# First batch's phi, keys and values as six tokens on each of 96 partitions, queries as pairs, one order on two engines; W1's means taken off by products

## The chip, the core and the metric

The kernel runs on one core of a Trainium2 chip. A core has TensorE (PE, matrix products into PSUM), VectorE (DVE), ScalarE (ACT), GpSimd (POOL) and SyncE (SP), whose queue here issues every load and store; 16 DMA engines carry them out. The metric is the device time of one execution in microseconds, the median of several runs.

## The reference

Three layers in a row, for 8 batches of 576 tokens. Attention over 32 memory slots a head, a layer norm with a two-layer network added to it, and a gated layer that mixes tokens:

```
a = softmax over the 576 tokens of phi          # 8 x 8 heads x 576 x 32
k_m, v_m = a^T k, a^T v                         # 32 x 64 a head
x = softmax(q k_m^T / 8) v_m                    # heads side by side: 576 x 512
xn = (x - mean(x)) / sqrt(var(x) + 1e-6) * g_ln
x = x + relu(xn @ w_ch1) @ w_ch2                # 512 -> 2048 -> 512
h = gelu(x @ w_in); u, v = halves of h          # 512 -> 1024
x + (u * (w_sg @ (layernorm(v) * g) + b_sg)) @ w_out
```

The weight matrices reach the chip as 64-bit floating-point numbers; q, k, v and phi are 32-bit.

## The kernel before

**Phase 1** takes the batches one behind the other; the second layer follows in phase 2, which the change does not touch. Since x is attention weights times v_m, the product of x with W1 is taken as attention weights times VW, where VW = v_m times W1. For that W1 is scaled by g_ln and its column means are taken off (`center_w1`: TensorE makes the means with a constant column, L505, DVE subtracts them in two instructions of 1024 elements a partition, L507). W1 has four quarters of 512 columns (`fb` 0 to 3), and the hidden layer runs quarter by quarter: six products make `ph` (L593, `m1`), ACT takes relu (`hh`, L579), DVE the rounding rest (`hl`, L580, and `cr` for the odd 64 tokens), and three steps later `m2` multiplies with W2 (L623 to L625).

**Weights** arrive as 64-bit words (`raw`, 128 x 512, runs of 4 KB). A tile is turned into 32-bit numbers by ACT on the upper words (L114) and DVE with a shift (L115) and a shift-or (L116). W1's are then scaled by ACT into `wc` (L499), W2's are split by ACT and GpSimd into a high and a low half (L128, L129). The centred W1 is stored to `w_d` by `store_w1` and read back by later batches (`load_wc`).

**The first batch** has nothing to stand beside. Phi, keys and values are loaded with 4 tokens a partition (512 of 576 tokens on 128 partitions, runs of 512 B) and a remainder of 64 tokens (`prz`, `kvr`). `prep_max` and `prep_exp` (L252 to L278) take the maximum over tokens with transposes on TensorE and the exponential; `prep_sum` adds four tokens and the remainder on GpSimd (L283 to L288) and `turn_sum` transposes the sums; `prep_kv` makes k_m and v_m (L315), `prep_norm` divides by the sums (L335), `prep_T` transposes them (L352). Queries are loaded token by token (runs of 256 B), transposed by TensorE (`t_q`, L376) and copied by ACT (L377). `t_scores` makes scores (L401), DVE transposes them (L410) and takes maxima and differences (L413, L414), ACT the exponential (L415); `t_norm` sums and divides (L421 to L424), `t_attn` transposes again (L429) and writes `aTh` and `aTl` (L440, L441). Tokens come in three groups: two of 256 and one of 64. `make_vw` multiplies v_m with W1 (L545), `evict_vw` splits the result (L551 on ACT, L552 on DVE).

**Order.** Each step is an event `at_time(time, function)` in units of an eighteenth of a batch; events with smaller times are issued earlier, those before -0.4 ahead of the first `ph`. A scheduler then sets each engine's order from the issue order and its own estimate; `tc.issue_after(x)` keeps an instruction behind x. All loads go by `load` (L87) on the SP queue in the issue order: an entry that waits for its buffer holds the ones behind it. From the second batch on, queries are laid out anew in DRAM (`q_d`, three buffers) and transposed by DVE (L379).

## Time and profile before

| | us |
|---|---|
| median of 3 runs | 1204.23 (1202.42 to 1206.30) |
| the profiled execution | 1205.68 |
| its span | 1203.50 |
| TensorE busy in the span | 1170.44 |
| DVE, ACT, GpSimd busy | 688.04, 467.69, 401.85 |

The profiled execution is one run, 1.45 us above the median; 2.18 us of it lie outside the span. All times in rows count from the span's start. Engine columns of a windows row are busy time with the number of instructions in brackets; a number in square brackets at a timeline row is the engine's idle time before it, with what ended it.

### The profile page before, as it was taken

To read this page: it belongs to the slowest core of one execution; us is meant where nothing else is said; L and a number is where in the kernel's file an instruction comes from. 1 tells how busy PE (TensorE), PEld (TensorE's weight loads), DVE (VectorE), ACT (ScalarE), POOL (GpSimd) and SP (SyncE) were. 2 spreads that over 40 slices of the span, in tenths; PEclk is the share of its full clock that TensorE was granted. 3 is DMA by queue.
4 is the path that set the end of the run, shared out by engine and by line. 5 is a ranking of instruction groups with operands and counts; after the bars stand their busy time and mean duration, and the time that the engine had idled before them with its cause. 6 is when DMAs were issued, how large, how long until landed. Compare 5 with 4: busy or idle time off the path is not lost.

```text
span 1203.5 us, 20688 instructions
## 1 busy us (share of the span) xinstructions
PE 1170.4 (97%) x7711; PEld 993.1 (83%) x7711; DVE 688.0 (57%) x1669; ACT 467.7 (39%) x1071; POOL 401.8 (33%) x622
## 2 busy tenths in 40 slices
PE   4899899999999999999999999999999999999998
PEld 3486678788788888788888888889989988998997
DVE  4886665755644645644546445567476377447532
ACT  3665332323332322422333445445444354344430
POOL 2234112311201211201211112456666475566641
PEclk9799899999999999999999999999999999999999
DMA  8984834463341543231410343032240052022201
GB/s 248 354 242 120 236 80 126 93 194 76 97 117 31 146 124 67 92 108 25 126 35 27 108 125 116 27 82 88 82 139 18 19 150 69 2 84 84 79 19 71
DMA packets 198900, 124.14 MB, mean 103 GB/s; under 512 B 93072, under 2 KB 174096, under 8 KB 198800
## 3 DMA queue, kind: packets, MB, share of 16 engines
q1 hardware_dynamic: 198800, 122.82, 35.4%
q8 instruction: 61, 1.00, 0.3%
q14 instruction: 39, 0.32, 0.1%
HBM read 99.72 MB, written 31.33 MB: 109 GB/s over the span
## 4 chain that ended last, share of the span: by engine, by line
PE 88%; DVE 6%; DMA 2%; SPq 1%; ACT 1%; issue 1%; POOL 1%; POOLq 0%; ACTq 0%; DVEq 0%
PE ph L593 16%; PE py L623 10%; PE py L625 10%; PE py L624 10%; PE pvs L1029 9%; PE po L1052 8%; PE pv L920 8%; PE pu L1004 7%; PE pvw L545 3%; DMA q<-q_d 1%; PE kvp L315 1%; SPq L87 1%; PE cm L505 1%; PE px L460 1%; DVE qT L379 1%; PE px L459 1%
## 5 line engine op out<-in xcount | busy, mean ns | idle before, releaser
L593 PE MATMUL ph<-aTh,vw 128*128 128x320 f32 (+1 forms) x1024 | 248.4, 301 | 1.4 <-ACT vw L551 1.4
L623 PE MATMUL py<-whl,hh 128*128 128x512 f32 x512 | 202.3, 397 | 6.7 <-ACT hh L579 6.5
L624 PE MATMUL py<-whl,hh 128*128 128x512 f32 x512 | 201.2, 393 | 0.0
L593 PEld LDWEIGHTS ph<-aTh,vw 128*128 128x128 f32 x1024 | 179.5, 191 | 26.0 <-issue 8.8
L625 PE MATMUL py<-whl,hl 128*128 128x512 f32 x512 | 182.7, 397 | 0.0
L579 ACT ACTIVATE hh<-ph 128x256 fp32r<-128x256 f32 x256 | 96.5, 386 | 168.5 <-PE ph L593 111.0
L580 DVE SCALAR_TENSOR_TENSOR hl<-ph,hh 128x256 fp32r<-128x256 f32 x256 | 106.4, 421 | 91.1 <-ACT hh L579 90.6
L593 PE MATMUL ph<-aTl,vw 128*128 128x256 f32 (+1 forms) x512 | 152.7, 299 | 0.0
L623 PEld LDWEIGHTS py<-whl,hh 128*128 128x128 f32 x512 | 96.5, 189 | 30.1 <-ACT hh L579 8.6
L1029 PE MATMUL pvs<-wsh,vhl 128*128 128x288 f32 x576 | 121.1, 295 | 0.0
L624 PEld LDWEIGHTS py<-whl,hh 128*128 128x128 f32 x512 | 96.7, 189 | 19.0 <-issue 0.5
L1004 PE MATMUL pu<-yTh,whl 128*128 128x288 f32 x512 | 111.0, 296 | 0.2 <-DVE ug L909 0.2
L593 PEld LDWEIGHTS ph<-aTl,vw 128*128 128x128 f32 x512 | 97.7, 191 | 11.2 <-issue 3.6
L625 PEld LDWEIGHTS py<-whl,hl 128*128 128x128 f32 x512 | 90.3, 190 | 11.9 <-issue 2.3
L1029 PEld LDWEIGHTS pvs<-wsh,vhl 128*128 128x128 f32 x576 | 94.4, 189 | 0.7
L920 PE MATMUL pv<-whl,yTh 128*128 128x512 f32 x288 | 91.0, 396 | 0.0
L1052 PE MATMUL po<-whl,gh 128*128 128x512 f32 x288 | 90.1, 391 | 0.0
L1004 PEld LDWEIGHTS pu<-yTh,whl 128*128 128x128 f32 x512 | 85.4, 189 | 1.9 <-DVE ug L909 0.9
L579 ACT ACTIVATE cr<-ph 128x64 fp32r<-128x64 f32 x128 | 28.7, 226 | 126.3 <-PE ph L593 125.7
L1032 POOL TENSOR_TENSOR gt<-gt,ug 128x288 f32<-128x288 f32 x64 | 52.9, 827 | 68.3 <-DVE gt L1031 61.8
L1029 PE MATMUL pvs<-wsl,vhl 128*128 128x288 f32 x256 | 75.6, 295 | 0.0
L1004 PE MATMUL pu<-yTl,whl 128*128 128x288 f32 x256 | 75.5, 295 | 0.0
(154 smaller groups left out, 2164.5 us busy)
## 6 DMA issues: line engine op xcount, KB each, us to landing
raw<-in_moe_w_ch_dram SPq DMA_DIRECT2D x32, 512.0 KB, 7.8
wc<-w_d SPq DMA_DIRECT2D x28, 512.0 KB, 5.7
y_d<-x SPq DMA_DIRECT2D x36, 256.0 KB, 2.2
yt<-y_d SPq DMA_DIRECT2D x36, 256.0 KB, 2.7
yr<-y_d SPq DMA_DIRECT2D x36, 256.0 KB, 2.8
kv<-in_k_dram SPq DMA_DIRECT2D x32, 256.0 KB, 3.9
kv<-in_v_dram SPq DMA_DIRECT2D x32, 256.0 KB, 4.0
out_dram<-yr SPq DMA_DIRECT2D x32, 256.0 KB, 2.0
```

Of the source, the lines that this page charges most:

```text
L545: mm = PE.matmul(ps[g][ms, :], vT[rs_, ms], ws[j // 2][rs_, j % 2, :], start=True, stop=True, skip_group_check=True)
L579: high = A.activation(out_h, src, AF.Relu)
L580: return high, V.scalar_tensor_tensor(out=out_l, in0=src, scalar=0.0, in1=out_h.bitcast(F32), op0=ALU.max, op1=ALU.subtract)
L593: R["ph"] = PE.matmul(ph, w_[:, ks], x[:, g, 0:w], start=(n == 0), stop=(n == 3 * HK - 1))
L623: PE.matmul(py, hh, wh, start=start, stop=False)
L624: PE.matmul(py, hh, wl, start=False, stop=False)
L625: PE.matmul(py, hl, wh, start=False, stop=stop)
L920: PE.matmul(pv, y[:, kc, cs], w, start=(n == 0), stop=(n == 3 * KC - 1))
L1004: PE.matmul(pu, w[:, ds_], y[:, kc, cs], start=(n == 0), stop=(n == 3 * KC - 1))
L1029: PE.matmul(pvs, v_, w_, start=(n == 0), stop=(n == len(ops) - 1))
L1032: G.tensor_tensor(out=gt, in0=gt, in1=ug, op=ALU.mult)
L1052: PE.matmul(po, gg[:, dc, cs], w, start=(n == 0), stop=(n == 3 * KC - 1))
```

## The change

Line numbers of the changed program differ. What it does:

- **Loads.** Batch 0's phi, keys and values come as 6 consecutive tokens on each of 96 partitions, with no remainder: phi in runs of 768 B, keys and values of 1536 B. Queries come as pairs of tokens (runs of 512 B), 256 tokens a load. The tiles lie in a pool of their own (`start`) that `open_tail` closes.
- **Sums.** TensorE adds the exponentials with the constant column (`kv_first`); GpSimd's sums and the transposes are gone.
- **Queries.** They are transposed by products with the identity that write 64 rows each; a strided copy puts the pairs in order.
- **One order.** `behind(gate)` chains the start's work on ACT (`st["act"]`) and DVE (`st["v"]`); the maximum and difference of the scores (`t_soft`) are a step of their own. The second group's query products wait for the first group's scores, the means for the second group's. Second and third group are divided by their sums behind the first VW.
- **Means.** For the first two quarters of W1, ACT writes the negated means (`ncm`) and TensorE adds v_m times `ncm` into the same sums as VW. DVE adds `ncm` to W1 later (`center_late`), ahead of the store. The last two quarters are centred as before, later in the order.
- **Weights.** The first four tiles of W2 are loaded ahead of W1's second quarter; the loads of the fourth quarter, the stores and the centring move to later times.

```diff
+    def behind(gate):
+        es = ExitStack()
+        for ins in gate or ():
+            es.enter_context(tc.issue_after(ins.ins))
+        return es
...
+        def load_kv0(g, n):
+            t = start.tile([P, 2, 2, C0, D], F32, name=f"kv0{g}{n}")
+            for i, src in enumerate((k, v)):
+                load(t[:P0, i], src[0, g, 2 * n:2 * n + 2].rearrange("h (p c) d -> p h c d", c=C0))
...
+        def kv_first(g):
...
+            for c in range(C0):
+                w = ex[:, c].rearrange("p h m -> p (h m)")
+                PE.matmul(st["sums"][:, g:g + 1], w, mcol[:P0], start=(c == 0), stop=(c == C0 - 1), skip_group_check=True)
...
+                elif i % 2 == 0:
+                    t = start.tile([P, H, 2, D], F32, name=f"q0{i}")
+                    load(t, q[b, :, i * P:i * P + 2 * P, :].rearrange("h (p r) d -> p h r d", r=2))
...
+                with behind([first_grs[n_ - 1]["sc"][0]] if n_ else None):
+                    for c in range(4):
+                        if n == P:
+                            for o in range(2):
+                                PE.matmul(pt[64 * o:64 * o + 64, c, :], t[:, 2 * c + o], ident, start=True, stop=True, skip_group_check=True)
...
         def center_w1(fb):
             ws = WC[fb]
             cm = ps_of(fb, [P, DM], "cm")
             for j in range(KC):
-                PE.matmul(cm, mean, ws[j // 2][:, j % 2, :], start=(j == 0), stop=(j == KC - 1))
-            for n in range(2):
-                V.tensor_tensor(out=ws[n], in0=ws[n], in1=cm.unsqueeze(1).to_broadcast([P, 2, DM]), op=ALU.subtract)
+                with behind([first_grs[1]["sc"][0]] if fb == 0 else None):
+                    PE.matmul(cm, mean, ws[j // 2][:, j % 2, :], start=(j == 0), stop=(j == KC - 1))
+            if fb < 2:
+                st["cm", fb] = at.tile([P, DM], F32, tag="at32" if fb else "z", name="ncm")
+                with behind([st["act"]] if fb == 0 else None):
+                    ins = A.mul(st["cm", fb], cm, -1.0)
+                if fb == 0:
+                    st["act"] = ins
+            else:
+                for n in range(2):
+                    V.tensor_tensor(out=ws[n], in0=ws[n], in1=cm.unsqueeze(1).to_broadcast([P, 2, DM]), op=ALU.subtract)
+
+        def center_late(fb):
+            with behind([st["hl"]]):
+                for ws in WC[fb]:
+                    V.tensor_tensor(out=ws, in0=ws, in1=st["cm", fb].unsqueeze(1).to_broadcast([P, 2, DM]), op=ALU.add)
...
+                    if late:
+                        for j in range(KC):
+                            for g in range(HK):
+                                rs_, ms = slice(64 * g, 64 * g + 64), slice(32 * j, 32 * j + 32)
+                                PE.matmul(ps[g][ms, :], vT[rs_, ms], st["cm", fb][rs_], start=False, stop=True, skip_group_check=True)
...
-            gate = st.get("hl", tiles[1 if c == 0 else 3]["tr"])
-            W2[c] = split([raws.pop(("w2", c))], wpool, gate=[gate])
+            W2[c] = split([raws.pop(("w2", c))], wpool, gate=[st["hl"]] if c > 3 else [st["v"], st["act"]])
+            if c < 4:
+                st["v"], st["act"] = R["word"], R["high"]
...
-            at_time((-16.5, -5.0, 3.0, 7.5)[fb], scale_w1, fb)
-            at_time((-16.4, -0.3, 4.6, 9.1)[fb], center_w1, fb)
-            at_time((-15, 1.3, 5.8, 10.3)[fb], make_vw, 0, [fb])
...
+                at_time((-25.7, -2.5, 4.0)[fb - 1], load_w1, fb, range(KC))
+                at_time((-5.0, 5.0, 8.6)[fb - 1], scale_w1, fb)
+            at_time((-17.9, -0.3, 5.0 + 1.6, 8.6 + 1.6)[fb], center_w1, fb)
+            at_time((-17.1, 1.3, 5.0 + 2.8, 8.6 + 2.8)[fb], make_vw, 0, [fb])
...
+            if fb < 2:
+                at_time((4.6, 7.6)[fb], center_late, fb)
+            at_time((4.7, 7.7, 9.5, 12.5)[fb], store_w1, fb)
```

DVE around the first VW (`z` are scores of a group, `r` their sums, `raw` weight words). Before:

```order
L424 TENSOR_TENSOR z_343<-z_343,r_409 128x512
L429 STREAM_TRANSPOSE z_343<-z_343 128x512
L421 TENSOR_REDUCE r_419<-z_360 128x16
L115 TENSOR_SCALAR raw<-raw 128x512
L422 TENSOR_SCALAR r_419<-r_419 128x16
L507 TENSOR_TENSOR wc<-wc,cm 128x1024 x2
L423 RECIPROCAL r_419<-r_419 128x16
L116 SCALAR_TENSOR_TENSOR raw<-raw 128x512
L424 TENSOR_TENSOR z_360<-z_360,r_419 128x512
L429 STREAM_TRANSPOSE z_360<-z_360 128x512
L421 TENSOR_REDUCE r_429<-z_377 128x4
L552 TENSOR_TENSOR vw<-pvw,vw 128x512
```

And after, with L511 the difference, L522 to L530 the division and transposition, L693 the split of VW, L724 `hl`:

```order
L511 TENSOR_TENSOR z_390<-z_390,m_393 128x512
L522 TENSOR_REDUCE r_411<-z_370 128x16
L523 TENSOR_SCALAR r_411<-r_411 128x16
L524 RECIPROCAL r_411<-r_411 128x16
L525 TENSOR_TENSOR z_370<-z_370,r_411 128x512
L530 STREAM_TRANSPOSE z_370<-z_370 128x512
L693 TENSOR_TENSOR vw<-pvw,vw 128x512 x2
L123 TENSOR_SCALAR raw<-raw 128x512
L124 SCALAR_TENSOR_TENSOR raw<-raw 128x512
L724 SCALAR_TENSOR_TENSOR hl<-ph,hh 128x256
```

The centring (L507) and the second group's division are gone from ahead of the first VW; the first group's maximum and division now stand together, and W2's first conversion comes behind VW.

DVE between the second and the third VW. Before, the third quarter's W1 is centred there:

```order
L467 BN_STATS s_908<-x 128x6
L116 SCALAR_TENSOR_TENSOR raw<-raw 128x512
L507 TENSOR_TENSOR wc<-wc,cm 128x1024 x2
L468 BN_AGGR mv<-s_908 128x2
L580 SCALAR_TENSOR_TENSOR hl<-ph,hh 128x256
L115 TENSOR_SCALAR raw<-raw 128x512
L470 TENSOR_SCALAR ve<-mv 128x2
```

And after, with L641 the late addition to W1's second quarter, L468 the next batch's query transposition, L352 and L355 its phi:

```order
L641 TENSOR_TENSOR wc<-wc,ncm 128x1024 x2
L468 STREAM_TRANSPOSE qT<-q 128x2x128
L724 SCALAR_TENSOR_TENSOR cr<-ph,cr 128x64
L352 TENSOR_TENSOR phi<-phi,mb 128x1024
L355 TENSOR_TENSOR prz<-prz,mb 64x128 x2
```

Two late additions and part of the next batch's preparation now stand ahead of the third quarter's conversions, its centring behind them.

The load queue around the fourth quarter (`q` is the tile that DVE transposes, `q_d` the laid-out queries, `wc` a quarter of W1 read back). Before:

```order
L87 DMA q<-q_d_99 128x512
L87 DMA q_d_99<-in_q_dram 512x1x32 x4
L87 DMA wc<-w_d_94 128x1024 x2
L87 DMA q<-q_d_97 128x512
L87 DMA kv<-in_k_dram 128x4x128
```

And after:

```order
L89 DMA q<-q_d_97 128x512
L89 DMA q_d_99<-in_q_dram 512x1x32 x2
L89 DMA q_d_97<-in_q_dram 512x1x32 x4
L89 DMA wc<-w_d_94 128x1024 x2
L89 DMA kv<-in_k_dram 128x4x128
```

The load from `q_d_97` now stands ahead of the two `wc` loads, the layout of the next queries between.

## Rows read from the trace of the kernel before

**Rows 1.** Windows by stage: length, busy PE, PEld, DVE, ACT, POOL; clock, DMA share, GB/s.

```profile
24.15:41.60 17.45, 11.16 (x40) 3.03 (x40) 16.92 (x36) 12.73 (x22) 2.47 (x2) 0.62 1.01 395
41.60:60.50 18.90, 16.83 (x67) 12.84 (x67) 15.56 (x34) 12.00 (x24) 4.09 (x4) 0.81 0.87 320
60.50:69.90 9.40, 9.40 (x66) 7.72 (x66) 7.05 (x17) 7.13 (x16) 0.00 (x0) 1.00 0.99 317
69.90:95.90 26.00, 24.80 (x137) 19.24 (x136) 21.56 (x54) 16.10 (x35) 9.21 (x15) 1.00 0.69 198
...
124.00:150.00 26.00, 21.52 (x156) 16.08 (x156) 17.95 (x49) 10.15 (x27) 5.27 (x8) 0.89 0.83 224
150.00:1203.50 1053.50, 1047.69 (x6913) 905.62 (x6897) 586.58 (x1432) 391.77 (x911) 360.99 (x562) 1.00 0.30 84
```

**Rows 2.** Timeline of the start: start us, us, what, [idle before].

```profile
11.43 6.14 SPq L87 DMA_DIRECT2D q<-in_q_dram  x5
...
41.61 0.58 PE L593 MATMUL ph<-aTh,vw 128*128 128x256 f32 x1 [0.69 <-ACT vw L551]
```

**Rows 3.** Chain that ended last, in order of time: start us, us, what.

```profile
18.28 5.87 DMA raw<-in_moe_w_ch_dram
...
36.68 1.13 DVE wc L507
37.86 3.13 PE pvw L545 x16
...
60.63 1.02 PE pvw L545 x16
...
69.94 0.71 PE ph L593 x6
```

**Rows 4.** Timeline of the third quarter's first rows.

```profile
95.93 0.28 PE L593 MATMUL ph<-aTh,vw 128*128 128x256 f32 x1
...
96.79 0.44 DVE L379 STREAM_TRANSPOSE qT<-q 128x256 f32<-128x256 f32 x1
...
97.14 1.18 DVE L271 TENSOR_TENSOR phi<-phi,mb 128x1024 f32<-128x1024 f32 x1
```

**Rows 5.** DVE's groups by form from 62.3 to 95.9 us: busy us, mean ns, idle before.

```profile
L116 DVE SCALAR_TENSOR_TENSOR raw<-raw 128x512 uint32<-128x512 uint32 x14 | 9.1, 687 | 0.0
L115 DVE TENSOR_SCALAR raw<-raw 128x512 uint32<-128x512 uint32 x14 | 5.9, 462 | 0.0
L580 DVE SCALAR_TENSOR_TENSOR hl<-ph,hh 128x256 fp32r<-128x256 f32 x11 | 4.6, 416 | 3.6 <-ACT hh L579 3.6
L507 DVE TENSOR_TENSOR wc<-wc,cm 128x1024 f32<-128x1024 f32 x2 | 2.3, 1207 | 0.0
...
L552 DVE TENSOR_TENSOR vw<-pvw,vw 128x512 fp32r<-128x512 f32 x3 | 2.0, 687 | 2.3 <-ACT vw L551 2.3
L580 DVE SCALAR_TENSOR_TENSOR cr<-ph,cr 128x64 fp32r<-128x64 f32 x7 | 1.5, 220 | 1.2 <-ACT cr L579 1.1
```

**Rows 6.** Timeline around 142 us: the load queue, DVE and TensorE.

```profile
135.17 1.04 SPq L87 DMA_DIRECT2D wc<-w_d  x2
...
142.20 1.08 DVE L379 STREAM_TRANSPOSE qT<-q 128x512 f32<-128x512 f32 x1 [3.61 <-DMA q<-q_d]
...
145.03 0.80 PE L623 MATMUL py<-whl,hh 128*128 128x512 f32 x1 [2.96 <-ACT hh L579]
...
146.90 0.47 PE L593 MATMUL ph<-aTh,vw 128*128 128x320 f32 x1
```

**Rows 7.** Windows of five us in the load phase, columns as in rows 1.

```profile
10.00:15.00 5.00, 3.89 (x46) 2.90 (x49) 2.93 (x8) 1.72 (x4) 1.12 (x2) 1.00 0.88 242
...
30.00:35.00 5.00, 4.77 (x6) 1.78 (x6) 4.96 (x12) 4.95 (x10) 0.00 (x0) 0.50 1.03 420
```

**Rows 8.** ACT's groups by form from 24.15 to 60 us.

```profile
L114 ACT ACTIVATE raw<-raw 128x512 f32<-128x512 f32 x17 | 11.3, 678 | 3.2 <-DMA raw<-in_moe_w_ch_dram 3.1
...
L551 ACT CAST vw<-pvw 128x512 fp32r<-128x512 f32 x2 | 1.1, 588 | 0.6 <-PE pvw L545 0.6
```

More of the change, by code (lines that the diff above doesn't have):

```diff
@@ L180, in load_phi, with norm_first @@
+        def norm_first():
+            rs = at.tile([P, 2], F32, tag="rs", name="rs")
+            with behind([R["word"]]):
+                V.tensor_scalar(rs, st["sums"], float(DM), 1e-9, op0=ALU.mult, op1=ALU.add)
+            V.reciprocal(out=rs, in_=rs)
+            st["rs", 0] = rs
+            for g in range(2):
+                prep_norm(0, g, st["kvp", 0][:, g])
         def load_phi(b, gs):
@@ L339, in prep_vb @@
             VBh, VBl = VBs[b % 2]
-            with tc.issue_after(st["kvT", b][1].ins):
+            with behind([st["act"] if b == 0 else st["kvT", b][1]]):
                 for j in range(4):
@@ L353, in prep_T @@
             kvT = at2.tile([P, 2, P], F32, tag="kvT", name="kvT")
-            st["kvT", b] = kvT, A.copy(kvT, pt)
+            with behind([st["act"]] if b == 0 else None):
+                st["kvT", b] = kvT, A.copy(kvT, pt)
+            st["act"] = st["kvT", b][1]
         aT = {}
@@ L408, in t_scores @@
                 z = at.tile([P, 4 * P], F32, tag="z", name="z")[:, 0:2 * w]
-            for g in range(2):
-                V.transpose(out=z[:, g * w:(g + 1) * w], in_=sc[g])
+            with behind([st["v"]] if b == 0 else None):
+                for g in range(2):
+                    V.transpose(out=z[:, g * w:(g + 1) * w], in_=sc[g])
             z3 = z.rearrange("p (b m) -> p b m", m=NM)
@@ L420, in t_norm @@
             r = at.tile([P, 16], F32, tag="r0", name="r0")[:, 0:nb]
-            V.tensor_reduce(out=r, in_=z3, axis=AX.X, op=ALU.add)
+            with behind([st["v"]] if gr["b"] == 0 else None):
+                V.tensor_reduce(out=r, in_=z3, axis=AX.X, op=ALU.add)
             V.tensor_scalar(r, r, 1e-9, None, op0=ALU.add)
@@ L491, in load_w1, with scale_w1, pre_w1, word_w1 @@
                 raws[fb].append(t)
-        def scale_w1(fb):
-            WC[fb] = ws = wc_tiles()
-            for j, raw in enumerate(raws.pop(fb)):
-                d = ws[j // 2][:, j % 2, :]
-                w = to_f32(raw, [st.get("hl", tiles[TB - 1]["tr"])] if fb else None)
-                A.activation(d, w, AF.Copy, scale=g1c[:, j:j + 1])
+        def scale_w1(fb, part=range(KC)):
+            if part[0] == 0:
+                WC[fb] = wc_tiles()
+            for j in part:
+                if fb == 0:
+                    w = words[j]
+                else:
+                    w = to_f32(raws[fb][j], [st["hl"], R["word"]] if "hl" in st else [first_grs[2]["ah"], st["v"], R["word"]])
+                with behind([st["act"]] if fb == 0 else None):
+                    ins = A.activation(WC[fb][j // 2][:, j % 2, :], w, AF.Copy, scale=g1c[:, j:j + 1])
+                if fb == 0:
+                    st["act"] = ins
+        words = {}
+        def pre_w1(j):
+            words[j] = words_of(raws[0][j])
+            with behind([st["act"]] if "act" in st else None):
+                st["act"] = upper(words[j])
+        def word_w1(j):
+            with behind([st["v"]] if "v" in st else None):
+                words[j] = lower(words[j])
+            st["v"] = R["word"]
         def center_w1(fb):
```

224 lines of the change are left out of this document (153 added, 71 removed).

## Prediction

> **What bounds the kernel now.** I read the windows by stage first, then the chain of waits in order of time, then the timeline around each step of that chain, and last the groups of VectorE (DVE) by form. The windows say where time can be won at all: after 150 us TensorE is busy 1047.69 of 1053.50 us at a granted clock of 1.00 [rows 1]. From row 1312 of TensorE's 5154, row 466 of DVE's 1490 and row 146 of the load queue's 429 the two programs issue the same rows in the same order, so the last three quarters change only in their starting time, and from 150 us to there TensorE has next to nothing to win. The question is how much earlier TensorE gets through that first part.
>
> There the reader is to see three things. (1) TensorE's own work of the batch begins at 41.61 with the first product of attention weights and VW (ph, L593) [rows 2]. Ahead of it the chain runs over the load queue (five query loads hold it from 11.43 for 6.14 us [rows 2]), the landing of W1's first part (issued at 18.28, 5.87 us on the way [rows 3]), and then DVE, busy 16.92 of the 17.45 us from 24.15 to 41.60 [rows 1]. The subtraction of W1's means (L507, 1.13 us a piece) stands last, and the VW products take 3.13 us, since the granted clock of that stretch is 0.62 [rows 1, 3]. (2) The second and third quarter of the hidden layer start at 69.94 and 95.93 [rows 3, 4]. Between them DVE is busy 21.56 of 26.00 us [rows 1] and waits mostly for ScalarE's (ACT's) halves: 3.6 us ahead of hl, 2.3 ahead of vw, 1.2 ahead of cr, 7.1 in all [rows 5]. (3) At 142 us a load of queries is late: DVE waits 3.61 us for it and TensorE then 2.96 us, after which the clock has fallen: a 128x320 product takes 0.47 us at 146.90 [rows 6], where one of 128x256 took 0.28 at 95.93 [rows 4], 0.35 by width. Of 26.00 us TensorE is busy 21.52 there, at a mean clock of 0.89 [rows 1].
>
> **Part 1: loads of the first batch.** From the shapes, phi is 0.59 MB, keys and values 2.36 MB, queries 0.52 MB for the first two groups, one raw tile of W1 0.52 MB. Before, most runs are 512 B: from 10 to 15 us 242 GB/s at a DMA share of 0.88, so 275 GB/s in full use. Runs of 4 KB (raw tiles, 30 to 35 us) make 420 at 1.03, so 408 [rows 7]. Per run and engine (16 of them) that is 29.8 and 161 ns; a line between the two gives 365 GB/s for 1536 B and 314 for 768 B. Phi 1.9 us, keys and values 6.5, queries 1.9, the first raw tile 1.3: 11.6 us from about 1.9 us. Since the first stretches do not fill the engines, I put the first raw landing at 15 and not 13.5, against 24.15: 9 us earlier. The bounds are 12 and, with all runs at 275 GB/s, 17.3 (2.3 later than I take). The third raw tile lands at about 19.5, the fourth at 20.8. The remainders (six loads) and GpSimd's sums vanish; the sums become six narrow products a group, beside the kvp products.
>
> The Trainium skill's "DMA: Bandwidth & Descriptors" (specifications table) has line rate from 512 B on; by that the longer runs would win nothing. The trace differs, 242 against 420 GB/s at similar shares [rows 7]; what the rule would make of the time is rival C. The same skill's "SBUF — State Buffer" (Door 1: The DMA port swizzle) speaks against 96 partitions, as two thirds of the bytes then go to half of the ports: by its 436 GB/s an estimate of 327, which would make the keys and values 7.2 us for 6.5. No run shows it, and the sum does without it.
>
> **Part 2: from W1's landing to the first ph.** After, DVE's rows from the third raw tile to the first transposed weights number 17; at the stretch's mean (16.92 us by 36, 0.47 [rows 1]) that is 8.0 us. 19.5 + 0.7 for ACT's upper words + 8.0 + 0.6 for ACT's copy gives 28.8 [rows 8]. On the other branch the fourth raw tile gives VW: the two subtractions (2.3 us) are gone from the path; in their place stand ACT's negated means (0.6, as vw's copy out of PSUM [rows 8]) and one more set of products of VW's size: 1.02 us at full clock [rows 3], 2.0 at half. I take half, since TensorE is fed as thinly as before. The first ph then comes at 29.6: 12 us earlier. Bounds: 31.9 with the slow loads, 27.5 with the early ones.
>
> **Part 3: first to second quarter.** The gain isn't kept. After, the softmax of the second and third group, four conversions of W2 and the four of W1's second part lie behind the first VW: 52 rows of DVE, at 0.43 us between the means of the two stretches (0.46 and 0.41 [rows 1]) 22.3 us, from about 31.0 to the second VW's halves. Dense, that ends at 53.3. But DVE waits on ACT at each half: from 41.60 to 60.50 it was busy 0.82 of the time, from 60.50 to 69.90 0.75 [rows 1]. At 0.8 it is 27.9 us, and the new single order puts four upper words of W1 (4 x 0.68 = 2.7 us [rows 8]) on ACT ahead of W2's second cast, for which DVE stands in line. 61.6, then the two halves: the second quarter begins at about 63.4, against 69.94, 6.5 us earlier. Covered there: the negated means of the second part and 1.02 us of products (paid on TensorE, counted in this).
>
> **Part 4: second to third quarter.** Between the two VWs DVE gets more: four late additions of 1024 elements (4 x 1.21 = 4.8 us [rows 5]) before the W1 stores, and of the next batch a query transposition (0.44), phi's subtraction (1.18 [rows 4]), two of the remainder (0.6) and three rows of sums (0.8), both estimates from cr's 0.22 and hl's 0.42 a row: 7.8 us. What goes is two conversions (0.46 + 0.69 each), three hl (0.42) and three cr (0.22): 4.2 us [rows 5]. From 26.4 us of work (62.4 to 95.9, less the 7.1 waited) it becomes 30.0. With DVE late, ACT's halves are there when it comes, so I take it nearly dense: 62.4 + 30.0 and 0.6 of waits is 93.0, against 95.93: 2.9 us earlier. The other end: at the busy share of before (0.83) 30.0 us take 36.1, which is rival D.
>
> **Part 5: the late query load.** On the load queue the load into q of the third buffer stood behind two wc loads, issued at 135.17, which wait for a buffer; it went behind them [rows 6]. After, it stands ahead of them, and DVE's transposition stands 27 rows behind the previous one and not 14. TensorE's 2.96 us of waiting and about 2.9 us of half clock (6 us of work that take 9) are the most to be had, 5.9. I take 5.0, since a shorter wait can stay for ACT's next half.
>
> **Sum:** 2.9 + 5.0 = 7.9 us; parts 1 to 3 are inside the 2.9. The profiled execution took 1205.68 (span 1203.50), so 1197.8; it lies 1.45 above the median of the runs, 1204.23, so the forecast is 1196.3.
>
> **Rivals.** A, *the early gain is kept.* If DVE stays dense behind the first VW (ACT's halves never late), the second VW is there at 53.3; TensorE needs 28.3 us for the first quarter (69.94 less 41.61), so it starts the second at 57.9 and the third 26.0 later, at 83.9; DVE's 53.3 + 30.0 is 83.3. At 84.5 it is 11.4 earlier, with part 5 16.4: 1187.8. For it speaks that DVE was busy 16.92 of 17.45 us where ACT was ahead; against it, the 7.1 us of waits in [rows 5].
>
> B, *the later waits take it back.* The late query load stays (its time hangs on the buffer's last reader, which moves with everything else), and only the 2.9 us remain: 1201.3, within the bound of no difference. For it: in a program whose queue order is so near, the same wait at another place costs the same.
>
> C, *runs move no faster.* The first raw tile lands 2.3 us later than taken, DVE follows, and of part 4's 2.9 us 0.9 remain: with part 5 a gain of 5.9, 1198.3. That is also where the Trainium skill's rule of part 1 leads. Against it: [rows 7].
>
> D, *slower: DVE between the second and third quarter.* DVE keeps its busy share of 0.83 there; the third quarter then waits until 62.4 + 36.1 and half a VW (0.7), 99.2, which is 3.3 us later than before; TensorE's clock falls in the gap as it did at 145 (2 us more), and the late query load stays. 5.3 later: 1209.5. It decides from a busy share of 0.90 (30.0 of 33.5 us), below which the third quarter comes later than before. For it: the late additions are DVE work that the first program did where TensorE had nothing to do. That the edit does not do what it says is excluded by the order: no subtraction stands ahead of the first VW.
>
> **How the numbers follow.** Forecast 0.42, A 0.18, C 0.08, B 0.20, D 0.12. What a measurement of this kernel can tell from no change is about 0.3%, 3.6 us: 1200.6 to 1207.8. Faster holds the forecast, A and C less a little for their spread across 1200.6: 0.66; no difference holds B and that spread: 0.22; slower is D: 0.12. The range runs from 1185 (A with the early end of part 1) to 1206 (B with the late query load and part 3's gain gone), leaving out D and a little below A, under 0.2.
>
> **What would show it.** The first ph near 29.6 proves parts 1 and 2, a landing of the first raw tile near 15 part 1 alone. A second quarter between 58 and 66 and a third between 88 and 97 prove parts 3 and 4; a third at 85 shows A, after 97 D. No wait of TensorE over 1 us and a clock of 1.00 between 124 and 150 us prove part 5. The forecast is wrong if a stretch after 150 us differs in length, if another load is late in its place, or if TensorE starts early but at half clock and stays there.

## The result, and the profile after

The changed kernel takes 1213.28 us (1212.84 to 1214.11, 6 runs), the kernel before 1203.92 (6 runs): ratio 1.0078, 95% interval 1.0065 to 1.0091. It is 9.4 us slower, where 7.9 faster was forecast. The profiled execution took 1213.04, its span is 1210.9.

| TensorE, us | before | forecast | after |
|---|---|---|---|
| first raw tile of W1 landed | 24.15 | 15 | 17.1 |
| first ph | 41.61 | 29.6 | 37.09 |
| second quarter's first ph | 69.94 | 63.4 | 71.78 |
| third quarter's first ph | 95.93 | 93.0 | 111.95 |
| VW products of the fourth quarter | 123.08 | | 136.54 |

TensorE begins 4.5 us earlier, is 1.8 late at the second quarter, 16.0 late at the third and 13.5 at the fourth; 7.4 of it are left at the end of the span. The windows after, cut at these places (length, then busy time of PE, PEld, DVE, ACT, POOL, granted clock, DMA share, GB/s), answer to [rows 1]:

```profile
0.00:37.10 37.10, 26.70 (x285) 18.27 (x285) 17.26 (x34) 13.96 (x23) 3.90 (x14) 1.00 1.01 332
37.10:71.80 34.70, 27.65 (x143) 19.76 (x143) 24.74 (x55) 23.73 (x51) 10.82 (x11) 0.90 0.73 222
71.80:112.00 40.20, 28.74 (x151) 20.36 (x151) 35.28 (x70) 21.91 (x44) 16.17 (x19) 0.95 0.61 176
...
124.00:150.00 26.00, 25.49 (x181) 18.86 (x180) 17.50 (x47) 10.74 (x28) 7.99 (x10) 1.00 0.73 202
```

The loss lies in the second and third row: TensorE is idle 7.1 of 34.7 and 11.5 of 40.2 us, where before it was idle 2.1 of 28.3 and 1.2 of 26.0. DVE is the reverse of what was hoped: up to the first ph it works 17.26 us of 37.1 (before, 23.7 of 41.6 us), and between second and third quarter 35.28 (before 21.56). The last row is the one part that went as forecast: no late query load, 25.49 of 26.00 us at full clock.

What TensorE waited for from the first ph on (engine, line, releaser: us in total, times, longest), after:

```profile
PE ph L737 <- DVE hl L724: 5.0, 3, 3.4
PE ph L737 <- ACT aTh L542: 4.7, 1, 4.7
PE pvw L680 <- DVE rs L382: 4.0, 1, 4.0
PE ph L737 <- ACT vw L692: 2.0, 3, 0.7
PE ptsum L378 <- POOL sm L369: 1.9, 1, 1.9
```

and the same view of the kernel before:

```profile
PE py L623 <- ACT hh L579: 6.5, 5, 3.0
PE cm L505 <- ACT wc L499: 1.8, 1, 1.8
PE ph L593 <- ACT vw L551: 1.4, 2, 0.7
```

Kinds of wait under 1 us in all are left out. The five kinds shown make 17.6 us, where three made 9.7 before; only ph's wait for ACT's vw is in both lists. The start, in the timeline after (start us, us, engine line op out<-in, [idle before <-releaser]):

```profile
10.28 2.72 PE L237 MATMUL sums<-mcol,ex 96*128 96x1 f32 x12 [1.23 <-ACT ex L228]
12.93 2.79 PE L240 MATMUL kvp<-kv,ex 96*32 96x128 f32 x48
15.65 2.72 PE L237 MATMUL sums<-mcol,ex 96*128 96x1 f32 x12
...
17.12 0.70 ACT L119 ACTIVATE raw<-raw 128x512 f32<-128x512 f32 x1 [6.03 <-DMA raw<-in_moe_w_ch_dram]
...
18.30 2.79 PE L240 MATMUL kvp<-kv,ex 96*32 96x128 f32 x48
...
21.01 2.69 PE L460 MATMUL ptq<-ident,q 128*64 128x128 f32 x32
...
22.89 0.63 ACT L466 COPY qT<-ptq 128x512 f32<-128x512 f32 x1 [5.06 <-PE ptq L460]
...
24.25 0.65 ACT L119 ACTIVATE raw<-raw 128x512 f32<-128x512 f32 x1
...
24.94 0.69 DVE L124 SCALAR_TENSOR_TENSOR raw<-raw 128x512 uint32<-128x512 uint32 x1 [3.17 <-ACT raw L119]
```

The first raw tile is there at 17.12. Then ACT stands still for 5.06 us, because the next thing in the single order is the copy of the first queries; these stand on TensorE behind sums and kvp products that fill it from 10.28 to 21.09. The second tile's upper words come at 24.25, and DVE waits for them with nothing else it may do.

The third quarter's VW, in TensorE's timeline after:

```profile
101.37 0.33 PE L378 MATMUL ptsum<-ident,sm 128*128 128x128 f32 x1 [1.85 <-POOL sm L369]
101.53 3.60 PE L627 MATMUL cm<-wc,mcol 128*128 128x512 f32 x8
104.97 0.27 PE L378 MATMUL ptsum<-ident,sm 128*128 128x128 f32 x1
109.27 1.96 PE L680 MATMUL pvw<-wc,kvT 64*32 64x512 f32 x16 [4.04 <-DVE rs L382]
111.95 0.58 PE L737 MATMUL ph<-aTh,vw 128*128 128x256 f32 x1 [0.71 <-ACT vw L692]
```

W1's means (cm) stand between the two transpositions of the second batch's sums (ptsum), which wait for GpSimd. DVE's order stands in the way as well: its subtraction of the means (L636) waits behind the conversions of other weights, and from 97.50 us to the start of VW DVE is busy 11.68 of 11.76 us (a windows row, then DVE's timeline):

```profile
97.50:109.26 11.76, 5.88 (x19) 2.97 (x19) 11.68 (x18) 5.69 (x9) 5.55 (x6) 0.94 0.83 257
```

```profile
105.57 0.69 DVE L124 SCALAR_TENSOR_TENSOR raw<-raw 128x512 uint32<-128x512 uint32 x1
...
106.17 2.35 DVE L636 TENSOR_TENSOR wc<-wc,cm 128x1024 f32<-128x1024 f32 x2
```

Before, VW was made at 90.78, ahead of that batch's exponential. The moved event times (means 6.6 for 4.6, VW 7.8 for 5.8) carried it past the batch's steps at 6.2 and 6.5, whose times stayed.

### The profile page after: what moved, and what is told of

Same layout as the page of the kernel before. It is cut to its first block, busy times and chain, and to the rows that moved or that the text cites. A ratio compares the mean times of both kernels' runs of the same rounds, so it can differ in the third digit from the quotient of the medians.

```text
span 1210.9 us, 20897 instructions
## 1 busy us (share of the span) xinstructions
PE 1176.2 (97%) x7829; PEld 999.6 (83%) x7829; DVE 692.8 (57%) x1664; ACT 468.4 (39%) x1071; POOL 401.6 (33%) x617
## 4 chain that ended last, share of the span: by engine, by line
PE 86%; DVE 7%; DMA 3%; ACT 2%; issue 1%; SPq 1%; POOL 1%; POOLq 0%; DVEq 0%; ACTq 0%
PE ph L737 16%; PE py L767 10%; PE py L769 10%; PE py L768 10%; PE pvs L1191 8%; PE po L1214 8%; PE pv L1082 8%; PE pu L1166 7%; PE pvw L680 3%; PE kvp L396 1%; DVE raw L124 1%; DMA raw<-in_moe_w_ch_dram 1%; PE sc L490 1%; DVE raw L123 1%; PE px L561 1%
## 5 line engine op out<-in xcount | busy, mean ns | idle before, releaser
L724 DVE SCALAR_TENSOR_TENSOR hl<-ph,hh 128x256 fp32r<-128x256 f32 x256 | 105.9, 420 | 86.5 <-ACT hh L723 85.7
L769 PEld LDWEIGHTS py<-whl,hl 128*128 128x128 f32 x512 | 90.5, 189 | 12.7 <-issue 2.3
L723 ACT ACTIVATE cr<-ph 128x64 fp32r<-128x64 f32 x128 | 28.3, 225 | 124.0 <-PE ph L737 123.6
```

The costliest lines, as they stand in the source:

```text
L723: high = A.activation(out_h, src, AF.Relu)
L724: return high, V.scalar_tensor_tensor(out=out_l, in0=src, scalar=0.0, in1=out_h.bitcast(F32), op0=ALU.max, op1=ALU.subtract)
L769: PE.matmul(py, hl, wh, start=False, stop=stop)
```

## Experiments

Unless a line says otherwise, diffs are against the changed kernel, and each was timed beside the kernel before on the same chip. VW 2, 3 and 4 are the starts of the VW products of W1's second to fourth quarter in the profiled execution, us.

| run | median | ratio to before (interval) | first ph | VW 2 | VW 3 | VW 4 |
|---|---|---|---|---|---|---|
| before | 1203.9 | | 41.6 | 60.6 | 90.8 | 123.1 |
| changed | 1213.3 | 1.0078 (1.0065 to 1.0091) | 37.1 | 69.1 | 109.3 | 136.5 |
| e1_times | 1213.2 | 1.0083 (1.0067 to 1.0100) | 37.1 | 74.3 | 99.5 | 128.9 |
| e2_no_late | 1211.7 | 1.0066 (1.0048 to 1.0084) | 37.7 | 69.6 | 107.6 | 134.7 |
| e3_start_alone | 1220.1 | 1.0138 (1.0118 to 1.0158) | 41.0 | 80.3 | 104.9 | 134.4 |
| e4_upper | 1215.0 | 1.0093 (1.0078 to 1.0108) | 37.6 | 68.8 | 110.9 | 138.5 |
| e5_sums1 | 1210.6 | 1.0053 (1.0032 to 1.0073) | 33.6 | 66.1 | 108.3 | 136.1 |
| e6_norm_early | 1213.6 | 1.0077 (1.0054 to 1.0099) | 40.6 | 69.5 | 110.2 | 137.1 |
| e7_means_alone | 1209.8 | 1.0045 (1.0027 to 1.0063) | 41.5 | 60.0 | 92.4 | 125.0 |
| e8_dma128 | 1213.0 (one execution) | | 38.1 | 70.1 | 110.3 | 137.1 |
| e9_fb2_first | 1217.5 | 1.0119 (1.0104 to 1.0134) | 38.2 | 70.1 | 104.9 | 138.9 |
| e10_sums_dve | 1211.9 | 1.0073 (1.0058 to 1.0088) | 33.8 | 66.3 | 107.8 | 136.1 |
| e11_both | 1214.4 | 1.0095 (1.0080 to 1.0110) | 33.4 | 65.9 | 101.8 | 134.8 |
| e12_gpsimd_adds | 1218.5 | 1.0129 (1.0112 to 1.0146) | 33.7 | 67.5 | 96.0 | 132.2 |
| e13_no_chain | 1214.3 | 1.0088 (1.0069 to 1.0108) | 47.1 | 56.5 | 108.6 | 138.4 |
| e14_w2_old | 1213.2 | 1.0083 (1.0065 to 1.0102) | 38.0 | 65.5 | 110.7 | 138.3 |
| e15_nochain_w2 | 1208.0 | 1.0038 (1.0025 to 1.0051) | 45.7 | 49.5 | 106.0 | 136.1 |
| e16_nochain_w2_times | 1206.5 | 1.0022 (1.0009 to 1.0034) | 47.4 | 57.5 | 88.8 | 122.2 |
| e17_first_only | 1204.6 | 1.0008 (0.9996 to 1.0020) | 45.4 | 56.1 | 90.6 | 119.1 |
| e18_start_no_chain | 1207.4 | 1.0029 (1.0017 to 1.0041) | 49.8 | 61.3 | 92.5 | 125.4 |

**Times or added work?** The first theory was that the moved event times cost the third quarter; the rival, VectorE's late additions.

```diff
-at_time((-25.7, -2.5, 4.0)[fb - 1], load_w1, fb, range(KC))
-at_time((-5.0, 5.0, 8.6)[fb - 1], scale_w1, fb)
+at_time((-25.7, -2.5, 2.0)[fb - 1], load_w1, fb, range(KC))
+at_time((-5.0, 3.0, 7.5)[fb - 1], scale_w1, fb)
...
+at_time((-17.9, -0.3, 4.6, 9.1)[fb], center_w1, fb)
+at_time((-17.1, 1.3, 5.8, 10.3)[fb], make_vw, 0, [fb])
...
+at_time((1.35, 2.9)[fb], center_late, fb)
+at_time((1.4, 3.0, 7.4, 12.0)[fb], store_w1, fb)
```

> The changed kernel with the old event times for W1's second to fourth quarter (conversion 3.0, 7.5; means 4.6, 9.1; VW 5.8, 10.3; loads and stores as before) and the late additions right behind the second VW and at 2.9. All work stays. If the moved times cost the stretch from second to third quarter (40.2 us against 26.0), it returns to 26 to 30 us and the time falls from 1213.3 to about 1203 (1200 to 1206). If the 4.8 us of late additions on VectorE cost it, wherever they stand, the time stays at 1210 to 1214.

The stretch from VW 2 to VW 3 falls from 40.2 to 25.2 us, as by the first theory, and the time does not move, as by the rival. Two of the four additions (at 42.59) now stand in the first quarter, which takes 41.3 us in place of 34.7, and the late query load is back, with TensorE's wait at 152.65:

```profile
152.65 0.80 PE L767 MATMUL py<-whl,hh 128*128 128x512 f32 x1 [2.97 <-ACT hh L723]
```

From 152.65 to 160.00 TensorE's mean granted clock is 0.78, between its two levels of 1.2 and 2.4 GHz. So the late load hangs on the event times, and the gain of part 5 came with the times that cost the third quarter; which of the moved times it is, no run tells apart.

```diff
 def center_late(fb):
     with behind([st["hl"]]):
         for ws in WC[fb]:
-            V.tensor_tensor(out=ws, in0=ws, in1=st["cm", fb]...to_broadcast([P, 2, DM]), op=ALU.add)
+            pass
```

> The changed kernel without the late additions of the means to W1 (4 instructions of 1.21 us on VectorE); the stored W1 of the first two quarters, and with it the later batches' result, lacks them. If VectorE's added work costs the stretch from second to third quarter, the time falls by 5 or more, to 1205 to 1208. If the moved event times cost it, by 0 to 3: 1210 to 1213.

This kernel leaves the additions out. It is 1.6 us faster, and the intervals of the two ratios overlap: the additions' work as such is the small part. Neither theory stood alone; the next cut was through the change itself.

**The two halves of the change.** The new start with the means undone and the old event times as in e1_times:

```diff
-if fb < 2:
+if fb < 0:
     st["cm", fb] = at.tile([P, DM], F32, tag="at32" if fb else "z", name="ncm")
...
-late = b == 0 and fb < 2
+late = False
...
-    at_time((4.6, 7.6)[fb], center_late, fb)
```

> The changed kernel with the part on the means undone: all quarters of W1 centred by VectorE ahead of VW and at the old event times; new loads, sums by products, one order on two engines stay. If the start (loads, one order) is sound and the means part is at fault, the first ph comes at 38 to 41 us and the time is 1198 to 1204. If the start is at fault, at least 1208.

And the kernel before with the means alone (negated means, products, late additions at 1.39 and 2.99; diff against the kernel before):

```diff
-for n in range(2):
-    V.tensor_tensor(out=ws[n], in0=ws[n], in1=cm.unsqueeze(1).to_broadcast([P, 2, DM]), op=ALU.subtract)
+if fb < 2:
+    st["cm", fb] = at.tile([P, DM], F32, tag="at32" if fb else "z", name="ncm")
+    A.mul(st["cm", fb], cm, -1.0)
...
+at_time((1.39, 2.99)[fb], center_late, fb)
```

> The kernel before with the part on the means alone: negated means by ScalarE, the products of VW's size on TensorE, the late additions on VectorE at 1.39 and 2.99, ahead of the stores; loads, sums and order as before. If the means part is a gain wherever it stands (it is worth 7 us on top of the new start), the first ph comes at about 39 for 41.6 and the time is 1198 to 1202. If it only helps where VectorE is late, it is 1202 to 1206.

Each half alone is slower than before: the start by 16.7 us, the means by 4.6 (1209.84 against 1205.26 on that chip). With the means the first ph does not move (41.5), VW 3 is 1.6 late, and the time lies above both expectations. The start is the dearer half, and the means take 6.8 of its 16.7 us off again.

**What in the start?** First the pieces that the timeline shows, one at a time.

```diff
-at_time((-20.2, -19.5, -18.08, -18.02)[j], pre_w1, j)
-at_time((-20.1, -19.0, -18.07, -17.95)[j], word_w1, j)
+at_time((-20.2, -20.15, -18.08, -18.02)[j], pre_w1, j)
+at_time((-20.1, -20.05, -18.07, -17.95)[j], word_w1, j)
```

> The changed kernel with the second raw tile's two conversions issued ahead of the first queries' copies in the single order (event times -20.15 and -20.05 for -19.5 and -19.0). If ScalarE's wait of 5.06 us behind the query copies holds up the start, the first ph moves from 37.1 to 34 to 36 us and the time falls by 1 to 3. If TensorE's sums and kvp products (busy from 10.3 to 21.1) set it, the first ph moves by less than 1 and the time by less than 1.

The first ph stays (37.6). ACT converts the second tile at 18.34 and then waits 4.11 us for the queries all the same, so it is not that tile's place that sets the start. TensorE's products come next.

```diff
-for c in range(C0):
+for c in range(1):
     w = ex[:, c].rearrange("p h m -> p (h m)")
-    PE.matmul(..., mcol[:P0], start=(c == 0), stop=(c == C0 - 1), ...)
+    PE.matmul(..., mcol[:P0], start=(c == 0), stop=(c == 0), ...)
```

> The changed kernel with the sums taken over one of the six tokens of each partition only (2 x 5 products left out, so the softmax of phi is divided by too little). The sums take TensorE 2 x 2.72 us ahead of the kvp products of each group. If they hold up the start, the queries' transposition moves from 21.0 to about 16.5, the first ph from 37.1 to about 33 and the time falls by 2 to 4. If ScalarE and VectorE set the start, the first ph moves by under 1 us and the time by under 1.

Here the sums cover one token in six. The first ph comes 3.5 us earlier, VW 2 3.0, VW 3 1.0. A version that keeps the sums whole does the same:

```diff
-for c in range(C0):
-    w = ex[:, c].rearrange("p h m -> p (h m)")
-    PE.matmul(st["sums"][:, g:g + 1], w, mcol[:P0], start=(c == 0), stop=(c == C0 - 1), ...)
+sm = at.tile([P, H, NM], F32, tag="z" if g else "kvn", name="sm")[:P0, 4 * g:4 * g + 4]
+V.tensor_reduce(out=sm, in_=ex.rearrange("p c h m -> p h m c"), axis=AX.X, op=ALU.add)
+PE.matmul(st["sums"][:, g:g + 1], sm.rearrange("p h m -> p (h m)"), mcol[:P0], start=True, stop=True, ...)
```

> The changed kernel with the first batch's sums over the six tokens made by VectorE (one reduction of 768 elements a group, about 1.3 us, where VectorE waits from 10 to 17 us) and one product a group in place of six. TensorE's 2 x 2.72 us fall to 2 x 0.5. If the sums by products cost the start 3.5 us, the first ph moves from 37.1 to 33 to 35; the third quarter stays at 110 to 112, set by the order, and the time falls by 1 to 3.

The first ph is at 33.8, the time 1211.9. The sums cost the start 3.3 us; of that the time shows 1.4, which is within the intervals. Then the loads, in a kernel that leaves out the last 64 tokens:

```diff
+G.memset(t[:, :, :, 4:C0, :], 0.0)
-load(t[:P0, i], src[0, g, 2 * n:2 * n + 2].rearrange("h (p c) d -> p h c d", c=C0))
+load(t[:, i, :, 0:4, :], src[0, g, 2 * n:2 * n + 2, 0:4 * P].rearrange("h (p c) d -> p h c d", c=4))
```

> The changed kernel with the first batch's keys and values loaded as 4 tokens (runs of 1024 B) on 128 partitions, without the last 64 tokens; the places of the missing tokens are set to zero, the products run over what lies there. From 2.5 to 15 us the changed kernel moved 261 to 287 GB/s at shares from 1.07 to 1.14. If 96 partitions hold it down, 128 move 310 or more. If runs of 0.5 to 1.5 KB move no faster per byte, it stays at 250 to 290.

Windows of 2.5 us in the load phase (same columns), after with 96 partitions and runs of 1536 B, then this run with 128 partitions and 1024 B:

```profile
5.00:7.50 2.50, 0.82 (x2) 0.37 (x2) 2.39 (x4) 0.00 (x0) 0.00 (x0) 1.00 1.07 261
7.50:10.00 2.50, 1.48 (x4) 1.00 (x4) 2.16 (x5) 0.61 (x1) 0.00 (x0) 1.00 1.08 261
10.00:12.50 2.50, 2.22 (x11) 2.22 (x11) 0.21 (x1) 1.07 (x2) 0.00 (x0) 1.00 1.10 265
```

```profile
5.00:7.50 2.50, 0.81 (x2) 0.36 (x2) 2.39 (x4) 0.00 (x0) 0.32 (x1) 1.00 1.06 363
7.50:10.00 2.50, 1.48 (x4) 1.00 (x4) 2.15 (x5) 0.58 (x1) 0.00 (x0) 1.00 1.08 374
10.00:12.50 2.50, 2.18 (x11) 2.18 (x11) 0.26 (x1) 1.11 (x2) 0.00 (x0) 1.00 1.15 331
```

At the same DMA share 261 to 265 GB/s become 331 to 374, though the runs are shorter: the 96 partitions hold the loads down. (The 287 GB/s of the expectation are not in the changed kernel; from 2.5 to 15 us it moved 261 to 279.) Yet the first raw tile, now there at 13.96, changes nothing: the first ph is at 38.1, and the one execution took 1213.0. The loads are not what the start waits for.

```diff
-at_time((-17.3, -16.3, -16.1)[gi], t_norm, gr)
-at_time((-17.2, -16.2, -16.0)[gi], t_attn, gr)
+at_time((-17.3, -17.15, -17.05)[gi], t_norm, gr)
+at_time((-17.2, -17.14, -17.04)[gi], t_attn, gr)
```

(with the third group's scores at -17.13 and its maximum at -17.06)

> The changed kernel with the second and third group's division, transposition and splits issued ahead of the first VW's copies and of W2's first conversion, as the order before had them (event times -17.15 and -17.14, -17.13 to -17.04). If the postponed groups hold up the first quarter (TensorE waits 4.71 us for aTh at 47.67 and runs at half clock to 53), that wait goes under 1.5, the second quarter comes at 65 to 68 for 71.8 and the time falls by 3 to 7. If W1's second part sets the second quarter, it stays at 70 to 72 and the time within 1.5 of 1213.

TensorE's wait of 4.71 us goes to 0.66, and 3.30 us stand ahead of the first ph in its place: VW 2 and the time are the same. The postponed groups are not at fault.

**The third quarter's order.**

```diff
-at_time((-17.9, -0.3, 5.0 + 1.6, 8.6 + 1.6)[fb], center_w1, fb)
-at_time((-17.1, 1.3, 5.0 + 2.8, 8.6 + 2.8)[fb], make_vw, 0, [fb])
+at_time((-17.9, -0.3, 6.1, 8.6 + 1.6)[fb], center_w1, fb)
+at_time((-17.1, 1.3, 6.15, 8.6 + 2.8)[fb], make_vw, 0, [fb])
```

(`evict_vw` with `make_vw`)

> The changed kernel with one thing moved: the means and VW of W1's third quarter at 6.1 and 6.15 for 6.6 and 7.8, which puts them ahead of the second batch's exponential and sums (6.2 and 6.5) in TensorE's order, as they were in the kernel before. If the third quarter stands at 112 because its means stand behind the next batch's sums (TensorE waits 1.85 us for GpSimd's sums at 101.37 and only then makes the means), it starts at 98 to 105 and the time falls by 4 to 9, to 1204 to 1209. If VectorE's work alone sets it, it stays at 109 to 112 and the time within 2 of 1213.

> The two edits together: sums by VectorE, and the third quarter's means and VW ahead of the second batch's exponential. If start and order are two causes in a row, the gains add up: first ph at 33 to 35, third quarter at 95 to 102, time 1201 to 1206. If one bound stands behind both (VectorE's work in the first 100 us), no more than the better of the two.

VW 3 does come earlier, at 104.9, and at 101.8 with DVE's sums, but the time gets worse by 4.2 and, against DVE's sums alone, 2.5 us. For e9_fb2_first that is outside both expectations. In e9_fb2_first TensorE has the means early, but DVE subtracts them only behind four more rows of conversion:

```profile
97.76 1.02 PE L627 MATMUL cm<-wc,mcol 128*128 128x512 f32 x2
...
98.79 1.81 DVE L124 SCALAR_TENSOR_TENSOR raw<-raw 128x512 uint32<-128x512 uint32 x1
...
102.05 2.34 DVE L636 TENSOR_TENSOR wc<-wc,cm 128x1024 f32<-128x1024 f32 x2
...
104.94 1.09 PE L680 MATMUL pvw<-wc,kvT 64*32 64x512 f32 x16 [2.06 <-DVE pvw L670]
```

From 130 to 170 us TensorE is busy 39.49 of 40 us in the changed kernel, 35.23 in e9_fb2_first and 33.37 in e11_both: the wait is moved, not removed. With the additions on GpSimd as well (`G.tensor_tensor` in `center_late`):

> As the run with both edits, and the late additions of the means on GpSimd instead of VectorE (4 instructions, by the 1.3 us that 512 elements take there 2.6 us each, where GpSimd is busy 9.5 of 26 us). If VectorE's added 4.8 us still stand in the stretch from second to third quarter, 2 to 4 us less than with both edits alone, 1198 to 1203. If GpSimd's work slows VectorE's or W2's low halves, the same or slower.

VW 3 stands at 96.0, the earliest of the runs with the single order, and 1218.5 is nearly the slowest time; TensorE is busy 31.05 of those 40 us.

**The single order.** Here the theory was that the chain of gates leaves DVE idle. All gates ahead of the first hl are dropped, with the chain also those that hold query products and means on TensorE behind the scores; the scheduler orders those instructions itself:

```diff
+FREE = [False]
 def behind(gate):
     es = ExitStack()
-    for ins in gate or ():
+    for ins in (gate or ()) if FREE[0] else ():
         es.enter_context(tc.issue_after(ins.ins))
...
     st["hl"] = R["relu"][1]
+    FREE[0] = True
```

> The changed kernel without the single order of the start: the gates that chain ScalarE's and VectorE's instructions ahead of the first hl are gone, the scheduler orders them by its own estimates as in the kernel before. VectorE was idle 19.8 of the first 37.1 us in the changed kernel; if the chain is what leaves it idle, W2's and W1's conversions move there, the first ph comes somewhat later (38 to 42), the second quarter at 62 to 67 for 71.8, and the time falls by 4 to 9 (1204 to 1209). If the order only trades one for the other, it stays within 3 of 1213.

W2's four tiles behind W1's second quarter again, with the chain otherwise kept:

```diff
-... else (-17.0, -15.9, -15.8, -15.7)[c]
+... else 0.9 * c - 4
-W2[c] = split([...], wpool, gate=[st["hl"]] if c > 3 else [st["v"], st["act"]])
+W2[c] = split([...], wpool, gate=[st["hl"]] if "hl" in st else [first_grs[2]["ah"], st["v"], R["word"]])
```

> The changed kernel with the first four tiles of W2 converted behind W1's second quarter again, at the old event times (0.9 c - 4), not chained between VW and W1's second quarter. If W2's place ahead of W1 holds up the second VW (69.1 us for 60.6 before), the second quarter starts at 65 to 69 for 71.8 and the time falls by 2 to 5. If W2's halves are then late for m2 (py), the waits move there and the time stays within 2 of 1213.

VW 2 comes 3.6 us earlier, at 65.5, and VW 3 stands at 110.7: the time stays.

Both pieces and DVE's sums:

> The two edits together and the sums by VectorE: new loads, no single order, W2 behind W1, means by products. If order and sums are what costs the start, 1200 to 1206. If the means part's work on VectorE (the late additions) still costs, 1206 to 1212.

Without the chain VW 2 is made at 56.5 (49.5 with all three), 13 to 20 us earlier; VW 3 is still at 108.6 (106.0). TensorE's timeline of e13_no_chain:

```profile
108.64 1.96 PE L682 MATMUL pvw<-wc,kvT 64*32 64x512 f32 x16 [4.64 <-DVE rs L384]
```

It is the row at 109.27 again. Of the three, only e15_nochain_w2 keeps something, 5.3 us.

Then with the means undone and the old event times: e18_start_no_chain is e3_start_alone without the chain (the two diffs together), e16_nochain_w2_times is that with W2's old place and DVE's sums, so that of the change the loads, the query products and the start's own event times are left.

> The new start alone (means undone, 1220.1 with the single order) without the single order; sums by products and W2 ahead of W1 stay. If the single order is what costs the start, 1207 to 1212. If the sums by products and W2's place cost it, 1215 or more.

> As that run, with the part on the means undone and the old event times for W1's quarters: what stays of the change is the loads (six tokens on 96 partitions, queries as pairs), the sums by VectorE and the query products. If the loads are a gain of their own once the order is the old one, the first ph comes at 36 to 39 and the time is 1195 to 1201. If VectorE's and ScalarE's work sets the first 100 us whatever lands when, 1201 to 1206.

1220.1 falls to 1207.4: the single order, with its gates on TensorE, costs 12.7 us there. From 40 to 60 us, e3_start_alone and then e18_start_no_chain:

```profile
40.00:60.00 20.00, 14.14 (x53) 11.37 (x50) 13.00 (x31) 9.96 (x22) 2.90 (x3) 0.62 0.47 145
```

```profile
40.00:60.00 20.00, 14.04 (x76) 8.14 (x75) 18.53 (x37) 13.86 (x28) 6.84 (x5) 0.91 1.02 372
```

With the chain TensorE runs 53 products at a mean clock of 0.62, DVE works 13.0 us and the DMA engines are half idle; without it, 76 at 0.91, 18.5 and busy. And this although the first ph comes later:

```profile
49.81 0.80 PE L739 MATMUL ph<-aTh,vw 128*128 128x256 f32 x2
```

8.9 us after that of e3_start_alone, 8.2 after that of the kernel before, and the program ends 12.7 us sooner than the one and 3.5 later than the other. What is left in e16_nochain_w2_times, the loads above all, is 2.4 us slower than before, interval 0.9 to 3.4 thousandths, so no gain, and just above both expectations.

At last the means for W1's first quarter only, on top of that:

```diff
-late = b == 0 and fb < 2
+late = b == 0 and fb < 1
...
+if fb < 1:
+    at_time(1.38, center_late, fb)
```

> As the run with the loads alone (no single order, W2 behind W1, sums by VectorE, old event times), with the means by products for W1's first quarter only, its late addition at 1.38 ahead of the store. TensorE waits 2.64 us there for VectorE's subtraction ahead of the first VW. If that wait is worth something where VectorE has room, the first ph comes 2 to 4 us earlier and the time is 1200 to 1204. If VectorE's added work takes it back, as in the kernel before with the means alone (4.6 us slower), 1205 to 1210.

1.0008 (0.9996 to 1.0020): no difference to the kernel before. No version ran faster than it.

## Why the prediction was wrong

**Part 1, loads.** Landing at 17.1 for 15, inside the bounds given (12 to 17.3), and at its late end. The step that failed is the line between two run lengths: it took 365 GB/s for 1536 B, and 261 to 265 were moved. It left out the partitions. Its end at 512 B was read low too: in the window of the 275 the query loads, with runs of 256 B, are issued from 11.43 on [rows 2]; ahead of them the kernel before moved 287 GB/s at a share of 0.98 with runs of 512 B, more than 96 partitions with 1536 B:

```profile
5.00:7.50 2.50, 0.00 (x0) 0.00 (x0) 0.57 (x1) 0.00 (x0) 0.00 (x0) 1.00 0.98 287
```

The rule of the Trainium skill that was set aside, "SBUF — State Buffer" (Door 1: The DMA port swizzle), speaks of this cause. The trace agrees in direction, 261 to 265 GB/s on 96 partitions against 331 to 374 on 128; the estimate of 327 worked out from the Trainium skill's figure was still too high. The Trainium skill's line rate from 512 B on ("DMA: Bandwidth & Descriptors", specifications table), which stood beside rival C, does not hold here: 128 partitions moved 287 at 512 B and 331 to 374 at 1024 B. None of this mattered to the time, since e8_dma128 had its first tile at 13.96 and gained nothing.

**Part 2, to the first ph.** 37.1 for 29.6. (The prediction adds up 28.8 for one branch and gives no sum for the other.) The sums "beside the kvp products" were costed at nothing with TensorE as cover, and TensorE had none: 2 x 2.72 us, of which 3.3 to 3.5 reach the first ph (e5_sums1, e10_sums_dve). The other 4 us lie, by the traces, in the path. The forecast counted DVE's rows behind the third raw tile; but e4_upper, which converts the second tile earlier, and e8_dma128, in which the first lands 3.2 us earlier, do not bring the first ph forward. It moves with the queries' transposition on TensorE (ptq): from there it is 16.1 us in the changed kernel (21.01 to 37.09) and 16.1 in e10_sums_dve (17.68 to 33.82). That path was not in the sum.

**Part 3.** 34.7 us from first ph to second quarter, forecast 33.8. The size was right, in part by luck: DVE worked 24.74 us of it where 22.3 were summed. The single order was costed at 2.7 us, and without it (e13_no_chain) VW 2 comes 9.4 us behind the first ph and not 32.0, though the first ph is 10 us later.

**Part 4** is where the sign went: 29.6 us were forecast, 40.2 measured. By stages the third quarter is 19.0 us later than forecast (111.95 for 93.0), 7.5 of it from part 2, 0.9 from part 3 and 10.6 from here. Two steps failed. First, DVE's work was mis-sized, 30.0 us for 35.28. It was dense, as was taken: up to VW 3 it was busy 35.21 of 37.46 us.

```profile
71.80:109.26 37.46, 26.73 (x134) 20.07 (x135) 35.21 (x69) 21.23 (x42) 16.17 (x19) 0.98 0.61 173
```

The conversions took longer than in [rows 5], by 3.1 us over these 24 rows (from 71.8 to 112 us):

```profile
L124 DVE SCALAR_TENSOR_TENSOR raw<-raw 128x512 uint32<-128x512 uint32 x12 | 9.9, 838 | 0.1
L123 DVE TENSOR_SCALAR raw<-raw 128x512 uint32<-128x512 uint32 x12 | 6.7, 570 | 0.0
```

Second, the sum did not read the order of steps. On TensorE W1's means had moved behind the second batch's sums, with a chain over ACT's exponential and GpSimd ahead of them; on DVE the subtraction had moved behind the conversions of other weights. The ten kernels with those moved times and the means in that place bear out that the order counts and not the beginning: the first ph lies anywhere from 33.6 to 47.1 and VW 2 from 49.5 to 70.1, and VW 3 stays at 106.0 to 110.9. Moving the means ahead on TensorE (e9_fb2_first, e11_both) wins 4.3 and 6.0 us of VW 3; DVE's order was not moved by itself in any run. One reading was mixed as well: the 7.1 us of waits beside DVE's 21.56 of 26.00 us belong to the longer stretch from 62.3 us on, for which part 4's sum uses them rightly.

**Part 5** was right: the wait is gone, 25.49 of 26.00 us. From VW 4, 13.5 us late, to the end, 7.4 late, 6.1 us are regained, where 5.0 were taken. e1_times and e18_start_no_chain, with the old times, have it back (2.97 and 3.25 us).

**The rivals.** D named the place (between second and third quarter), the sign and the point from which it decides: DVE's busy share there is 35.28 of 40.20, 0.88, below the 0.90. But its mechanism, DVE waiting as before, is not what happened: up to VW 3 the share is 0.94, and the work itself was longer. Its price was a fifth of the real one, 3.3 us late for 16.0, and its late query load did not stay. That it had the sign right is luck in that part. B, C and A fell with part 4.

**What causes the 9.4 us.** Two things, each of which is enough by itself for a slower kernel:

| | with the single order | without |
|---|---|---|
| means by products, moved times | 1213.3 (changed) | 1214.3 (e13_no_chain) |
| means by DVE, old times | 1220.1 (e3_start_alone) | 1207.4 (e18_start_no_chain) |

Undoing one leaves the other: without the chain VW 3 stays at 108.6, with the old times the chain holds VW 2 at 80.3. Undo both and 5.9 of the 9.4 us are back. The means part, products and moved times together, costs 6.9 us without the chain and gives 6.8 back with it. This is shown. With the chain the two can be told apart: at the old times the products give 6.9 us (e1_times against e3_start_alone), and the moved times, the additions' among them, give and take nothing (1213.3 against 1213.2). Without the chain no run separates them; products for the first quarter alone, at the old times, cost nothing there (e17_first_only). Nor does a run separate the chain on DVE and ACT from the gates on TensorE. That the means' place in TensorE's order holds up VW 3 is shown by e9_fb2_first and e11_both for 4.3 and 6.0 us of it; that the time depends on it alone is refuted by the same runs. What turns an earlier VW 3 into waits between 130 and 170 us in e9_fb2_first, e11_both and e12_gpsimd_adds stays open; no run tells apart the four parts of that stretch (the fourth quarter's conversions, the second batch's VW, its queries, GpSimd).

## What to carry to other kernels

An earlier first matmul is no gain where the engines that feed it are not ahead: e18_start_no_chain starts TensorE 8.9 us later than e3_start_alone and ends 12.7 us earlier; from 40 to 60 us DVE works 18.5 us there for 13.0. Before a step is moved to a later time, look at what stands between the two places in the order of each engine that the step uses, not only of the busiest one, and what the step itself then stands behind. And count the rows that a chain over two engines holds back: here it was written to make an order certain and costed at 2.7 us, and with the means by DVE it cost 12.7.
